# A linear-attention kernel with a feed-forward layer: another order of its opening, other due times, and sums of k times v with 48 weight columns

## The chip, the cores and the metric

The kernel runs on one core of a Trainium2 chip. The metric is the device time of one execution in microseconds (us). The five engines of the core are TensorE (PE in the profile, its weight loads PEld), VectorE (DVE), ScalarE (ACT), GpSimd (POOL) and SyncE (SP), which here issues the DMAs.

## The reference

Four batches (B), eight heads (H), 768 positions (S) and head size 48 (D). First a gated recurrence for each batch and head, then a feed-forward layer with squared relu on 3072 tokens, model size 384 and inner size 2048:

```python
state = np.zeros((B, H, D, D))
for t in range(S):
    state = alpha[:, :, t, :, None] * state + np.einsum('bhd,bhe->bhde', k[:, :, t], v[:, :, t])
    y[:, :, t] = np.einsum('bhd,bhde->bhe', q[:, :, t], state)
x = y.transpose(0, 2, 1, 3).reshape(B * S, H * D)
h = np.maximum(x @ w_in, 0.0)
out = h * h @ w_out
```

The inputs of the recurrence are float32; the two weight matrices come as 8 bytes a number and are converted to float32 in the kernel.

## The kernel before, in words

**Blocks.** The recurrence is cut into chunks of 128 positions. A block n is one chunk of one batch; there are 24 blocks, and four of them (one chunk of all four batches) make a group g, so there are six groups. The feed-forward layer runs on a group of 512 tokens at a time.

**Attention of a block.** `ln` takes the logs of alpha and `cs` (L288 to L292) sums them along the chunk on TensorE. `eb` and `ei` make the exponentials b and 1/b, and `mq`, `mk` (L314) multiply q and k with them. `qT`, `kT` (L355), or `turn` (tile T, L529) for later groups, transpose them on TensorE; `qc`, `kc` copy the result out (L371, L537). `scores` (sc, L418) forms the products of q and k, `state_sums` (kv, L441) the sums of k times v, both into the same two PSUM banks (tile `sckv`). `masked` (am, L426) and `sums_copied` (us, L452) take them out on VectorE, `next_state` (st, L466 and L467) forms the new state, scaled with the last row of b. For the first four blocks that row is turned on TensorE (`lt` L343, `lc` L349); for later ones it goes through memory: `bl` stores it and `br` (L333) loads it as tile `last`, both from SyncE's queue. The output y of two blocks (L398) is made in `ga` and `gb`, which also hold scores, sums, masks and the new state of the next two blocks: `ga` those of its first, `gb` those of its second. `ev` copies y into the columns of x (L562, on ScalarE, for a few on VectorE). Two heads share a tile of 128 rows: head e = 0 has rows 0 to 63, head e = 1 has rows 64 to 127; of each 64 only D = 48 are numbers of that head, the rest are zeros or unused.

**Feed-forward of a group.** Group 0 multiplies in plain float32: L931 for h (`ha`, `hb`: the two halves of the tokens), and L760 for the output. Later groups split weights and x into a near and a rest part and multiply in three passes (L681 for h; L843 and L855, in part still L760, for the output). The parts of the weights are made once (`prepare`), stored, and loaded again for each group; `room` bounds how many such tiles are held at a time. ScalarE and VectorE work up h: relu and square (L696, L594, L710 and others).

**Weights.** `load_weights` (L122 on SyncE) brings a raw piece of 768 KB; `convert_first` (L174, L178 on VectorE), `convert_middle` (L187, L190 on ScalarE) and `convert_second` (L196, L200, L203 on VectorE) turn it into float32. Words such as `first0`, `middle0` and `second0` in the order stand for these for piece 0.

**What sets the order.** Nothing is scheduled by a program at build time: each engine runs its instructions in the order in which the Python code records them. For the first four blocks and the first pieces of weights that order is a string of step names, recorded word by word. A word such as `load2a` issues a DMA on SyncE; words of different engines only order work that shares an engine. `zeros` records three float32 matmuls of zeros (L384) into a bank that nobody reads. After the string, `weave` mixes units of feed-forward work, each with a cost, with events that have a due time in the same units: the attention steps of later blocks, loads, weight splits. An event is recorded ahead of the first unit that begins at or after its due time. The due times are in the table `AT` and, relative to the start of a pair of blocks, in `PLAN`.

```python
def weave(units, events, at=0):
    for cost, f, args in units:
        while events and events[0][0] <= at:
            _, e, given = events.pop(0)
            e(*given)
        f(*args)
        at += cost
```

Of the kernel before, what the change touches and what calls it, by code (L numbers as in the profile page):

```python
# [15 lines left out]


GB = 4
AT = {'u0': 2, 'evs': 0.4, 'lead': 4, 'post': 3, 'w_first': (45.82, 44.44, 94.99), 'wstep': 2.31, 'w_in_at': 1.92, 'w_in_by': 3.02, 'room1': 25, 'room': 26, 's0': 3, 'ahead': 12, 'late': 23, 'xs': 0.35, 'g0': (-0.17, 20.59, 27.02), 'sc0': (2.36, 2.26, 2.42), 'g1': (7.68, 18.74, 27.21), 'g': (2.3, 15.42), 'g1x': 47.42, 'gx': 39.86, 'g0x': 55.51, 'k0': 2, 'h0': 16, 'k1': 5, 'h1': 0, 'h1by': 5, 'evs0': 0.23, 'tp': 'DDAD', 'tp1': 'AADD', 'split': 8, 'o0': (42.39, 46.35), 'o1': (), 'o2': (21.54, 19.65, 30.49, 26.1, 43.38, 50.96), 'str1': 14.0, 'ga': 9.32, 'gb': 12.97}


RUN = {0: 128, 32: 32, 64: 64, 96: 32}
# [3 lines left out]
def kernel(  # L26
# [13 lines left out]
    B, H, S, D = q.shape  # L40
    C = 128
    NCH = S // C
    NP = H // 2
# [4 lines left out]
    G = 64 - D  # L48
# [19 lines left out]
    s_t = [s_all.pop(0) for _ in range(B)]  # L68
# [30 lines left out]
    def tile_of(x, n):  # L99
        return lent.get((x, n), tiles[x][n % len(tiles[x])])  # L100
# [133 lines left out]
    last = consts.tile([128, 4, NP], FP32, name="last")  # L234
    nc.gpsimd.memset(last, 0.0)
    last_t = [last[:, i, :] for i in range(4)]
# [33 lines left out]

    SPLIT = AT["split"]

# [135 lines left out]
    HALF = [slice(0, 64), slice(64, C)]  # L408
# [26 lines left out]
    def state_sums(n):  # L435
        ps = two[n]
        for p in range(NP):
            for e in range(2):
                first = (2 * p + e) * D
                for h in range(1 if n // B == NCH - 1 else 2):  # L440
                    marks["k", n] = nc.tensor.matmul(  # L441
                        out=ps[h][64 * e : 64 * (e + 1), 1, p, G:64],
                        lhsT=tile_of("k", n)[HALF[h], 2 * p + e, :],
                        rhs=tiles["v"][n % NV][HALF[h], first : first + D],
                        start=True, stop=True, skip_group_check=True,
                    )

    def sums_copied(n):

        ps = two.pop(n)  # L450
        u = blk[n]["u"] = u_all[n % 3]
        nc.vector.tensor_tensor(  # L452
            out=own(u), in0=own(ps[0][:, 1]), in1=own(s_t[n % B]), op=ALU.add
        )
        blk[n]["kv1"] = own(ps[1][:, 1])

    def own(x):
        return x[:, :, G:64]

    def next_state(n):  # L460
        blk[n]["s"] = s_t[n % B]
        if n // B < NCH - 1:
            s_all.append(s_t[n % B])
            s_t[n % B] = s_all.pop(0)
            s, last = own(s_t[n % B]), last_t[n % 4].unsqueeze(2).to_broadcast([128, NP, D])
            nc.vector.tensor_tensor(out=s, in0=blk[n].pop("kv1"), in1=own(blk[n]["u"]), op=ALU.add)  # L466
            nc.vector.tensor_tensor(out=s, in0=s, in1=last, op=ALU.mult)  # L467

# [17 lines left out]
    def ga(a, n):  # L486

        if n is not None:
            for f in (scores, state_sums, masked, sums_copied):
                f(n)  # L490
        if a is not None:
            product = y_begin(a)
            for h in range(1 if a < B else 0, 2):
                for m, p, e in heads(a):
                    rows = slice(64 * e, 64 * e + D)
                    s = blk[m]["u" if h else "s"]
                    product(m, p, e, s[rows, p, G * (1 - e) : 64], blk[m]["qs"][rows, p, HALF[h]], HALF[h])


            for m, p, e in heads(a):  # L500
                end = inner(product, m, p, e, e)
            marks["y", a] = end
            passed = nc.gpsimd.nop(nofuse=True)
            dep(passed, end)
            two["y"] = product, passed
        if n is not None:
            next_state(n)

    def gb(a, n):

        if a is not None:
            product, passed = two.pop("y")
            for i, (m, p, e) in enumerate(heads(a)):
                begin = inner(product, m, p, e, 1 - e)
                if i == 0:
                    dep(begin, passed)
        if n is not None:
            for f in (scores, state_sums, masked, sums_copied, next_state):
                f(n + 1)
# [67 lines left out]
    here, todo, room = {}, [], [22]  # L587
# [37 lines left out]
    def diff_w(w, p):  # L625
# [7 lines left out]
        for x in "ld":  # L633
            t = made.pop((x, w, p))
            if w == "i" or p >= NW - AT["k0"] or (x == "l" and p >= NW - AT["k1"]):
                here[x, w, p] = t
        pump()

    def prepare(at, w, p):
        step = AT["wstep"]  # L640
        fs = (cast_w, rest_w, diff_w)
        return [(at + i * step, f, (w, p)) for i, f in enumerate(fs)]
# [78 lines left out]
    def splits_of_x(at, g):  # L721
        return [(at + i * AT["xs"], f, (g, i % KM)) for i, f in enumerate((split_x,) * KM + (diff_x,) * KM)]

    def layer_in(g):
        units = []
        for n in range(NJ + 2):
            if n < NJ:
                units.append((1.05, in_x, (n,)))
            if 0 <= n - 2 < NJ:
                units.append((0.53, in_y, (n - 2,)))  # L730
            if 0 <= n - AT["post"] < NJ:
                units.append((0, in_post, (n - AT["post"],)))
            if AT["lead"] <= n < AT["lead"] + AHEAD and (g > 1 or AT["k1"] == NW):
# [230 lines left out]

    steps = {f.__name__: f for f in (ln, sp, cs, eb, ei, mq, mk, bl, br, lt, lc, qT, qc, kT, kc, ev)}
    steps["sc"], steps["kv"], steps["am"] = scores, state_sums, masked
    steps["us"], steps["st"] = sums_copied, next_state
    steps["ya"], steps["yb"] = lambda n: ga(n, None), lambda n: gb(n, None)
# [5 lines left out]
    for x in "stky":  # L974
# [3 lines left out]
    steps["hb"] = lambda j: ffn_in(0, j, slice(HT, 2 * HT))  # L978
    steps["first"], steps["middle"], steps["second"] = convert_first, convert_middle, convert_second
    first = """  # L980
        zeros2 ln0 cs0 ln1 eb0 cs1 load0v ei0 mq0 mk0 load2a eb1 qT0 load3a qc0 mq1
        kT0 kc0 load1v ei1 qT1 mk1 load2k load2q qc1 sc0 kT1 weights0 kc1 kv0 load3q
        am0 lt1 sc1 ln2 us0 ln3 cs2 lt0 am1 load3k kv1 cs3 eb2 us1 ei2 gt1 mk2
        load2v weights1 ya0 mq2 yb0 lc1 gy0 eb3 kT2 lc0 load3v qT2 ei3 load4a zeros2
        st0 ea00 kc2 qc2 ed01 ed02 first0 zeros2 load4q mq3 zeros2 mk3 qT3 middle0
        qc3 kT3 second0 first1 kc3 lt3 lt2 sc2 kv2 am2 ea03 us2 sc3 kv3 gk3 middle1
        weights2 lc3 am3 us3 ha0 ya2 yb2 second1 weights3 ea20 lc2 ed21 ha1 ha3
        weights4 ed22 ed23 first2 st2 middle2 ha2 hb0 load4v hb1 st3 st1 load4k
    """
    for word in first.split():  # L990
        f = max((x for x in steps if word.startswith(x)), key=len)
# [2 lines left out]


    PLAN = (
        (-1.2, "ln0 ln1"),
        (-0.5, "sp0"),
        (0.0, "sp1"),
        (2.5, "cs0 cs1 eb0 ei0"),  # L1000
        (3.0, "eb1 ei1"),
        (3.5, "mk0"),
        (4.0, "bl0"),
        (4.5, "mq0 mk1 bl1"),
        (5.0, "mq1"),
        (6.5, "turn br1"),
        (7.0, "kc0 qc0 kc1 qc1 br0"),
        (9.5, "ga"),
        (10.5, "gb"),
    )  # L1010
    EARLY = (
        (0, "ln0"),
# [90 lines left out]
    for g in range(1, NG):  # L1103
        events = []
        if g + 1 < NG:
            n = GB * (g + 1) + 2
# [4 lines left out]
        if g == 1:  # L1111
# [5 lines left out]
            n = min(AT["k0"], AT["k1"])  # L1117
# [41 lines left out]
```

## Time and profile before

| | us |
|---|---|
| Median of 3 runs | 516.4 (515.83 to 516.55) |
| Span of the profiled execution, first to last instruction | 514.6 |
| TensorE busy | 508.3 |
| VectorE busy | 377.0 |
| ScalarE busy | 302.3 |
| GpSimd busy | 6.0 |

The profile holds one execution. Its own time is not listed beside it, only its span; the median lies 1.8 us above the span, and times in the text are made from the span and that difference. The mean granted TensorE clock was 1.000. The busy time of TensorE is the time in which at least one matmul was in flight; it does not say that each matmul is as short as it can be, and zeros count as busy like any other matmul.

A row of the chain in time has its start, its length, and the engine, tile and line (and x, the number of instructions). A row of the timeline has start, length, engine, line, operation, output <- input, shapes and count. A row of the groups has busy time, mean ns of one instruction, then idle time before it and what ended it. A row of the waits has who waited for whom: us in total, times, and the longest in us. A float32 matmul shows as two records of TensorE, except in the small tiles of scores, sums and y, where 16 matmuls show as 32.

### The profile page before, as it was taken

What the parts mean: (1) busy time and instruction counts of PE and PEld (TensorE: products, weight loads), DVE (VectorE), ACT (ScalarE), POOL (GpSimd) and SP (SyncE); (2) the same over time, 40 slices, a digit from 0 to 9 for tenths busy, and PEclk for the clock granted to TensorE, in tenths of its full rate; (3) what the DMA queues carried; (4) which work ended last, traced back from release to release, by engine and by line L of the source; (5) the groups of instructions that cost most, each with busy time, mean ns of one, the idle gap of its engine ahead of it and who ended that gap; (6) DMA issues with size and microseconds to landing.
All of it is one profiled execution on the core that took longest, in us unless ns stands there. A gap on an engine that the chain in (4) does not pass through costs nothing.

```text
span 514.6 us, 12773 instructions
## 1 busy us (share of the span) xinstructions
PE 508.3 (99%) x5166; PEld 404.6 (79%) x5166; DVE 377.0 (73%) x656; ACT 302.3 (59%) x627; POOL 6.0 (1%) x33
## 2 busy tenths in 40 slices
PE   8999999999999999999999999999999999999997
PEld 6884456669877679988888888888888888888996
DVE  3798899898789869886698286799275588274961
ACT  4789875677788576376764175855075663144520
POOL 4000000000000000000000000000000000000000
PEclk9999999999999999999999999999999999999999
DMA  9989867272797788799975678894775544789201
GB/s 171 226 238 269 233 177 226 33 224 101 267 238 199 189 188 234 263 330 222 241 187 154 209 220 229 222 225 146 227 221 168 186 128 151 214 277 401 88 0 63
DMA packets 144794, 102.73 MB, mean 200 GB/s; under 512 B 116560, under 2 KB 118240, under 8 KB 144736
## 3 DMA queue, kind: packets, MB, share of 16 engines
q1 hardware_dynamic: 144736, 101.92, 70.4%
q8 instruction: 41, 0.67, 0.6%
q14 instruction: 17, 0.14, 0.1%
HBM read 84.57 MB, written 17.33 MB: 198 GB/s over the span
## 4 chain that ended last, share of the span: by engine, by line
PE 96%; DMA 2%; SPq 1%; DVE 1%; issue 0%; ACT 0%; DVEq 0%; POOLq 0%
PE h L681 31%; PE o L760 22%; PE o L843 13%; PE h L931 8%; PE o L855 6%; PE y L398 4%; PE sckv L418 3%; PE T L529 2%; PE sckv L441 2%; PE cs L288 1%; DMA a_in<-in_alpha_dram 1%; PE zeros L384 1%; DMA last<-row 1%; PE cs L291 1%; SPq L333 1%; PE cs L292 1%
## 5 line engine op out<-in xcount | busy, mean ns | idle before, releaser
L696 ACT ACTIVATE hid<-h 128x512 f32<-128x512 f32 x56 | 33.7, 601 | 88.4 <-PE h L681 86.7
L681 PE MATMUL h<-xd,wd 128*128 128x512 f32 x240 | 68.4, 398 | 0.0
L681 PE MATMUL h<-xa,wb 128*128 128x512 f32 x240 | 67.8, 391 | 0.0
L681 PE MATMUL h<-xl,wl 128*128 128x512 f32 x240 | 67.6, 390 | 0.0
L594 DVE TENSOR_TENSOR hid<-h,hid 128x512 f32<-128x512 f32 x56 | 38.5, 689 | 33.9 <-PE h L681 33.6
L562 ACT COPY x<-y 32x256 f32<-32x256 f32 (+1 forms) x137 | 48.9, 365 | 8.7 <-PE y L398 6.4
L681 PEld LDWEIGHTS h<-xl,wl 128*128 128x128 f32 x240 | 45.0, 188 | 9.6
L681 PEld LDWEIGHTS h<-xa,wb 128*128 128x128 f32 x240 | 44.9, 188 | 9.4
L681 PEld LDWEIGHTS h<-xd,wd 128*128 128x128 f32 x240 | 43.7, 188 | 9.2
L760 PE MATMUL o<-w_out,hid 128*128 128x384 f32 x144 | 48.9, 492 | 0.0
L931 PE MATMUL h<-x,w_in 128*128 128x512 f32 (+1 forms) x120 | 43.0, 511 | 0.0
L655 ACT ACTIVATE ha<-hid 128x512 fp32r<-128x512 f32 x42 | 26.7, 638 | 26.1 <-DVE hx L656 12.8
L760 PEld LDWEIGHTS o<-w_out,hid 128*128 128x128 f32 x144 | 26.7, 190 | 17.2
L710 DVE SCALAR_TENSOR_TENSOR hid<-hid 128x512 f32<-128x512 f32 x56 | 37.8, 684 | 0.0
L931 PEld LDWEIGHTS h<-x,w_in 128*128 128x128 f32 x120 | 22.4, 190 | 16.9 <-issue 13.9
L855 PE MATMUL o<-hd,wd 128*128 128x512 f32 x144 | 33.4, 391 | 0.0
L656 DVE SCALAR_TENSOR_TENSOR hl<-ha,hid 128x512 fp32r<-128x512 f32 x42 | 28.8, 686 | 4.7 <-ACT ha L655 4.4
L855 PEld LDWEIGHTS o<-hd,wd 128*128 128x128 f32 x144 | 26.8, 188 | 6.1 <-ACT o L848 0.6
L594 DVE TENSOR_TENSOR hd<-ha,hl 128x512 fp32r<-128x512 f32 x42 | 29.1, 692 | 1.9
L843 PE MATMUL o<-hx,wb 128*128 128x512 f32 x72 | 28.4, 394 | 0.0
L843 PE MATMUL o<-hx,wl 128*128 128x512 f32 x72 | 28.0, 389 | 0.0
L843 PE MATMUL o<-ha,wb 128*128 128x512 f32 x72 | 28.0, 389 | 0.0
(130 smaller groups left out, 950.4 us busy)
## 6 DMA issues: line engine op xcount, KB each, us to landing
wd<-do SPq DMA_DIRECT2D x37, 384.0 KB
wl<-lo SPq DMA_DIRECT2D x34, 384.0 KB
wl<-li SPq DMA_DIRECT2D x32, 384.0 KB
wd<-di SPq DMA_DIRECT2D x32, 384.0 KB
raw<-in_moe_w_in_dram SPq DMA_DIRECT2D x8, 768.0 KB
raw<-in_moe_w_out_dram SPq DMA_DIRECT2D x8, 768.0 KB
v_in<-in_v_dram SPq DMA_DIRECT2D x24, 192.0 KB
a_in<-in_alpha_dram SPq DMA_DIRECT2D x22, 192.0 KB
```

The costliest lines, as they stand in the source:

```text
L398: ins = nc.tensor.matmul(out=ys[e][64 * half : 64 * half + D + G * e, m % 2, p // 2, t], lhsT=lhsT, rhs=rhs, start=(half, e) not in seen, ...
L562: copy(out=x[kk][to : to + m, t : t + 2], in_=blk[n]["y"][e][r : r + m, :, p // 2],)
L594: nc.vector.tensor_tensor(out=o, in0=x, in1=z, op=op)
L655: nc.scalar.activation(out=a, in_=x, func=AF.Copy, scale=NEAR * E)
L656: nc.vector.scalar_tensor_tensor(out=l, in0=a.bitcast(FP32), scalar=-1.0 / E, in1=x, op0=ALU.mult, op1=ALU.add)
L681: nc.tensor.matmul(out=acc["h", j], lhsT=here[w, "i", p][:, kk, jj * 128 : (jj + 1) * 128], rhs=x_parts[x][:, kk], start=start and kk == 0 ...
L696: nc.scalar.activation(out=hid[j], in_=x, func=AF.Copy, scale=E)
L710: nc.vector.scalar_tensor_tensor(out=h, in0=h, scalar=0.0, in1=h, op0=ALU.max, op1=ALU.mult)
L760: nc.tensor.matmul(out=acc[t][:, 0:DM], lhsT=lhs[:, t * C : (t + 1) * C], rhs=rhs, start=start, stop=stop, skip_group_check=True,)
L843: nc.tensor.matmul(out=acc[c], lhsT=by_parts(here[w, "o", p], jj, c), rhs=x, start=n == 0 and w == "b", stop=n == NJ - 1 and w == "l", ski ...
L855: nc.tensor.matmul(out=acc[c], lhsT=by_parts(here["d", "o", p], n % 2, c), rhs=h_diff[n], start=False, stop=last and n == NJ - 1, skip_gro ...
L931: nc.tensor.matmul(out=ps, lhsT=w[:, kk, c0 : c0 + 128], rhs=xT[g][kk][:, cols], start=(kk == 0), stop=(kk == KM - 1),)
```

## The change

- **The opening's string.** The same steps in another order, with two words `zeros2` less (four become two, so twelve filler matmuls become six). The loads of SyncE come in the order a0 q0 k0 a1 q1 k1 v0 v1 q2 a2 a3 k2 raw0 q3 k3 raw1 v2 v3 a4 raw2; before it is a0 q0 k0 a1 q1 k1 v0 a2 a3 v1 k2 q2 raw0 q3 k3 v2 raw1 v3 a4 q4 raw2. `first1` now comes before `second0`.
- **Due times.** Many values of `AT` and five rows of `PLAN` change: among them `turn` from 6.5 to 6.99, `ga` from 9.32 to 10.09 and the bounds `room1` and `room` from 25 and 26 to 24.
- **The sums of k times v.** The second head of a pair (e = 1) takes 48 columns of k as weights instead of 64, so it writes rows 64 to 111 instead of 64 to 127. VectorE's steps on the sums and states (L452, L466, L467) take 112 partitions instead of 128.

```diff
-AT = {'u0': 2, 'evs': 0.4, 'lead': 4, 'post': 3, 'w_first': (45.82, 44.44, 94.99), 'wstep': 2.31, 'w_in_at': 1.92, 'w_in_by': 3.02, 'room1': 25, 'room': 26, 's0': 3, 'ahead': 12, 'late': 23, 'xs': 0.35, 'g0': (-0.17, 20.59, 27.02), 'sc0': (2.36, 2.26, 2.42), 'g1': (7.68, 18.74, 27.21), 'g': (2.3, 15.42), 'g1x': 47.42, 'gx': 39.86, 'g0x': 55.51, 'k0': 2, 'h0': 16, 'k1': 5, 'h1': 0, 'h1by': 5, 'evs0': 0.23, 'tp': 'DDAD', 'tp1': 'AADD', 'split': 8, 'o0': (42.39, 46.35), 'o1': (), 'o2': (21.54, 19.65, 30.49, 26.1, 43.38, 50.96), 'str1': 14.0, 'ga': 9.32, 'gb': 12.97}
+AT = {'u0': 2, 'evs': 0.5, 'lead': 5, 'post': 3, 'w_first': (41.0, 46.62, 98.0), 'wstep': 2.4, 'w_in_at': 1.95, 'w_in_by': 2.89, 'room1': 24, 'room': 24, 's0': 2, 'ahead': 11, 'late': 23, 'xs': 0.13, 'g0': (-0.17, 20.59, 27.32), 'sc0': (2.35, 2.26, 2.45), 'g1': (6.25, 18.12, 27.21), 'g': (2.83, 13.94), 'g1x': 50.81, 'gx': 38.48, 'g0x': 56.05, 'k0': 2, 'h0': 15, 'k1': 5, 'h1': 2, 'h1by': 7, 'evs0': 0.29, 'tp': 'DDAD', 'tp1': 'AADD', 'split': 8, 'o0': (40.99, 48.51), 'o1': (), 'o2': (21.44, 19.65, 30.49, 28.56, 43.81, 48.78), 'str1': 15.07, 'ga': 10.09, 'gb': 12.97}
...
-                first = (2 * p + e) * D
+                first, wide = (2 * p + e) * D, D if e else 64
...
-                        out=ps[h][64 * e : 64 * (e + 1), 1, p, G:64],
-                        lhsT=tile_of("k", n)[HALF[h], 2 * p + e, :],
+                        out=ps[h][64 * e : 64 * e + wide, 1, p, G:64],
+                        lhsT=tile_of("k", n)[HALF[h], 2 * p + e, 0:wide],
...
     def own(x):
-        return x[:, :, G:64]
+        return x[0 : 64 + D, :, G:64]
...
-        zeros2 ln0 cs0 ln1 eb0 cs1 load0v ei0 mq0 mk0 load2a eb1 qT0 load3a qc0 mq1
-        kT0 kc0 load1v ei1 qT1 mk1 load2k load2q qc1 sc0 kT1 weights0 kc1 kv0 load3q
-        am0 lt1 sc1 ln2 us0 ln3 cs2 lt0 am1 load3k kv1 cs3 eb2 us1 ei2 gt1 mk2
-        load2v weights1 ya0 mq2 yb0 lc1 gy0 eb3 kT2 lc0 load3v qT2 ei3 load4a zeros2
-        st0 ea00 kc2 qc2 ed01 ed02 first0 zeros2 load4q mq3 zeros2 mk3 qT3 middle0
-        qc3 kT3 second0 first1 kc3 lt3 lt2 sc2 kv2 am2 ea03 us2 sc3 kv3 gk3 middle1
-        weights2 lc3 am3 us3 ha0 ya2 yb2 second1 weights3 ea20 lc2 ed21 ha1 ha3
-        weights4 ed22 ed23 first2 st2 middle2 ha2 hb0 load4v hb1 st3 st1 load4k
+        zeros2 ln0 ln1 cs0 eb0 cs1 ei0 mq0 load0v eb1 mk0 qT0 ei1 load1v mq1 qc0 kT0 load2q
+        load2a load3a kc0 qT1 mk1 load2k weights0 lt1 sc0 kT1 qc1 load3q kc1 am0 kv0 ln2
+        ln3 lt0 sc1 kv1 cs2 am1 us0 us1 cs3 ei2 gt1 load3k eb2 weights1 eb3 lc1 load2v ya0
+        yb0 lc0 gy0 ei3 load3v mk2 kT2 mq2 first0 qT2 ea00 load4a st0 kc2 qc2 weights2 mq3
+        lt3 ed01 qT3 zeros2 ed02 middle0 mk3 load4q kT3 lc3 first1 second0 kc3 load4v qc3
+        ea03 middle1 lt2 sc2 kv2 sc3 kv3 am2 ha0 us2 am3 us3 gk3 second1 ya2 yb2 weights4
+        lc2 ea20 ed21 ha1 ed22 ed23 st2 load4k weights3 first2 middle2 ha3 ha2 st1 hb1 hb0
+        st3
...
-        (-1.2, "ln0 ln1"),
-        (-0.5, "sp0"),
-        (0.0, "sp1"),
+        (-1.84, "ln0 ln1"),
+        (-0.24, "sp1"),
+        (0.22, "sp0"),
...
-        (4.5, "mq0 mk1 bl1"),
+        (4.37, "mq0 mk1 bl1"),
...
-        (6.5, "turn br1"),
+        (6.99, "turn br1"),
...
-        (10.5, "gb"),
+        (10.25, "gb"),
```

More of the change, by code (lines that the diff above doesn't have):

```diff
@@ L464, in next_state @@
             s_t[n % B] = s_all.pop(0)
-            s, last = own(s_t[n % B]), last_t[n % 4].unsqueeze(2).to_broadcast([128, NP, D])
+            s, last = own(s_t[n % B]), last_t[n % 4][0 : 64 + D].unsqueeze(2).to_broadcast([64 + D, NP, D])
             nc.vector.tensor_tensor(out=s, in0=blk[n].pop("kv1"), in1=own(blk[n]["u"]), op=ALU.add)
```

## Prediction

> **What bounds the kernel now.** I read the page's head first, then the chain in time through the opening, the opening's timeline, the groups by form, and at last the waits.
>
> ```profile
> PE 508.3 (99%) x5166; PEld 404.6 (79%) x5166; DVE 377.0 (73%) x656; ACT 302.3 (59%) x627; POOL 6.0 (1%) x33
> PEclk9999999999999999999999999999999999999999
> PE 96%; DMA 2%; SPq 1%; DVE 1%; issue 0%; ACT 0%; DVEq 0%; POOLq 0%
> ```
>
> TensorE is the path: it is busy 99% of the span at the full granted clock, and 96% of the chain is its own work. So an edit counts only where it takes PE work away, or a stretch in which PE stands or is kept busy with filler. The chain in time shows that the opening has such filler:
>
> ```profile
> 18.92 3.89 PE zeros L384 x18
> ...
> 24.29 0.62 PE sckv L418 x32
> ...
> 25.37 0.48 PE sckv L418 x32
> ...
> 26.30 1.49 PE h L931 x6
> ```
>
> The zeros row is work whose output nobody reads. The next rows of the timeline show what runs beside it:
>
> ```profile
> 20.00 0.54 DVE L174 TENSOR_SCALAR power<-raw 128x768 uint32<-128x768 uint32 x1
> 24.09 0.96 DVE L203 TENSOR_TENSOR w_in<-w_in,power 128x768 f32<-128x768 f32 x1
> 24.97 0.55 DVE L174 TENSOR_SCALAR power<-raw 128x768 uint32<-128x768 uint32 x1
> 26.02 0.78 DVE L426 COPY_PREDICATED am<-halves_mask,sckv 128x256 f32<-128x256 uint32 x2
> ```
>
> The first FFN matmul (26.30) needs the weights that L203 ends at 25.05, and the y of blocks 2 and 3 needs the masks from 26.02 on. VectorE is the second path of the opening, right behind PE.
>
> **Zeros.** Six of the twelve filler matmuls go, all from this run (nine become three): twelve of its 18 records, 12 x 0.216 (3.89/18) = 2.59 us. That is a gain only if the first FFN matmul and the masks come earlier, which VectorE decides; so the next part carries the price.
>
> **The opening's order.** Up to about 16 us I walk the new order with the old durations: am0 now lies ahead of kv0, which starts at 12.1 for 11.66; sc1, kv1, cs2 and cs3 then follow each other at their old lengths and the first y starts at 15.97, before 15.91. No cost: the transposes of the row sums (lt) went into a PE gap. a2 and a3 land some 2 us later (three 192 KB loads at about 1.0 us each stand ahead, two of them were behind), about 13 and 14; cs2 and cs3 begin after 14, so that is covered, with under 1 us to spare.
> From 18 us VectorE is laid end to end. The first part of raw0's conversion (L174, L178) can start at 18.24, as raw0 lands at 18.19 (before it was started at 20.00). Then st0, mq3, three x copies (1.33), mk3 and lc3 follow, to 22.35. Now the order has L174 and L178 of **raw1** ahead of the second part of raw0 (L196, L200, L203): 0.46 + 0.56 + three at 0.88 to 0.96, so L203 ends t + 3.80, t being the later of 22.35 and raw1's landing. Before raw1 was issued at 17.92 and landed at 24.36; now its issue follows k3 directly, near 14.2, and v2 is behind it. k3 landed at 19.76; raw0 and raw1 added 2.5 to 3.5 us each to the load ahead of them. So raw1 lands at 22.3 to 23.3, and the first FFN matmul starts at 26.2 to 27.1, before 26.30 (26.23 in the timeline). am2 keeps its place behind L203, so y moves with it. Bounds: -0.1 and +0.9 us; a wait of 0.2 us on the x copies at 34.6 us falls away if all comes later. I take +0.5, the middle, since raw0 was nearer 3.5 on its slowest part and 2.5 on most. So the 2.59 us are not gained: they turn into PE time without filler, 18 to 26 us.
>
> **The narrow weights.** 704 sums matmuls become half 64, half 48 columns wide. What a narrower load is worth shows in y, which already mixes both:
>
> ```profile
> L441 PEld LDWEIGHTS sckv<-v_in,k_in 64*64 64x64 f32 x672 | 13.2, 135 | 0.2 <-issue 0.2
> L398 PEld LDWEIGHTS y<-am,v_in 64*64 64x64 f32 x384 | 13.5, 134 | 0.0
> L398 PEld LDWEIGHTS y<-am,v_in 64*48 64x48 f32 x384 | 12.6, 120 | 4.2 <-issue 3.7 <-POOLq L503 0.5
> ```
>
> One 48-column load takes 120 ns, one of 64 134: 14 ns less. But the tiles of the array load side by side, each at a pace of its own: in a run of y at 16.5 us the 64-wide pair begins a load every 58 ns, the 48-wide pair beside it every 56, and the run ends with the slower. So it spans 422 ns from first to last load, as do the all-64 scores (423); these sums take 428. The change narrows one pair of the sums (e = 1) and leaves the other. [...] I take 0, the y rows being nearest. VectorE's 112 partitions for 128 save nothing: x copies of 16, 32, 48 and 64 partitions take 361 to 367 ns alike.
> [...]
>
> **Attention steps of later groups.** The new due times join two sections of group 1:
>
> ```profile
> 67.86 0.62 PE sckv L418 x32
> 68.48 0.45 PE sckv L441 x32
> 68.94 2.77 PE h L931 x6
> 71.71 0.63 PE sckv L418 x32
> ```
>
> Now the second pair follows the first, and the six matmuls of h come after. By the starts in the timeline, scores to second sums take 4.36 us (67.79 to 72.15), 1.79 without 2.57 for h; the same three runs side by side in the opening take 1.45 (24.22 to 25.67). Gain 0.35 us (0 if the steps are split again elsewhere). All other sections only move between matmuls of the same kind.
> What is left are waits of PE. Before has three that a move touches: at 144.2 the transposes T stand 0.20 us for q times b (L314, 144.00 to 144.55); nine L681 matmuls now lie between, some 2 us, so it goes. At 181.5 T stands 0.4 us for the bank that the x copies (L562, to 182.2) empty; T comes two L760 (0.65 us) later, the copies are 0.1 unit further apart, so 0.4 goes. At 238.2:
>
> ```profile
> DVE s L467 <- DMA last<-row: 10.0, 3, 4.2
> ```
>
> ```profile
> 233.06 3.86 DMA last<-row
> ...
> 237.31 0.68 DVE hid L710
> 238.00 0.61 DVE hid L594
> 238.61 0.04 issue
> 238.66 0.68 PE sckv L418 x28
> ```
>
> VectorE's state step waits for a row that comes through memory; behind it queue two FFN steps, and the scores need the bank that the second one empties: 0.45 us. The step (in ga) moves from 9.32 to 10.09 units, past such FFN steps, while the row's DMAs (br0) stay at 7.0: they run before the wait, and 0.45 goes. Each of these is 0 to its full length: together 0 to -1.05, taken in full, as in the rows around I find the released work early enough. Of moves that I cost at nothing (weight splits w_first, o0, o2; casts; loads; 24 kept tiles for 26), ScalarE (59%) and VectorE (73%) have room, and each us of a late step would be a PE us.
>
> **Sum.** 0.5 - 0.35 - 1.05 = -0.9 on a span of 514.6: 513.7. The three runs have a median of 516.4, 1.8 above the profiled span; so 515.5. About 0.2% (1.03 us) is what a measurement of this kernel tells from no change, and 515.4 is the line for faster.
>
> **Rivals.**
> - Early raw1: it lands by 22.8 or before, the opening costs 0 to +0.2, and the time is about 515.0. For: most parts of raw0 took 2.5 us. With the forecast this is one mechanism; 0.26 here, 0.31 for raw1 late (515.2 to 515.9).
> - The narrow loads pay: -2.05 more, 513.5. For: the 14 ns. Against: the 64-wide pair sets the pace. 0.10.
> - The conversion isn't last: if only 0.8 of the 2.59 us of filler comes back, because the walk has VectorE too late, -0.9 - 0.5 - 0.8 = -2.2, 514.2. Against: each VectorE row there is back to back. 0.08.
> - Slower, the rows: place, SyncE's queue ahead of the state steps. The DMAs of a row pass the weight streams, whose issue waits for a free tile, and 24 tiles for 26 in the later groups makes those waits longer. The three waits above total 10.0 with a longest of 4.2, so near 4.2, 2.9, 2.9; PE lost 0.45 at the longest, so the cover is 3.75. With every row 1.5 us later they are 5.7, 4.4, 4.4 and cost 1.95 + 0.65 + 0.65 = 3.25. In place of the -0.45 that is +2.8: sum +2.35, 518.8. It decides from 1.1 us on, where the sum passes +1.0. For: the row's first DMA stood 1.92 us in SyncE's queue at 230.1. Against: ga's later place gives 1 us more cover. 0.20.
> - Slower, the clock: PE now stands in pieces of up to 1.9 us between 18 and 26 us. At the start matmuls of this size begin every 427 ns (1.7 to 5.5 us), in the long run of filler every 216. A fall to half speed that lasts as long as it did there, 4.4 us, over the first FFN run and y (1.49 + 1.42 + 0.69 and what follows) costs half of it, 2.2: sum +1.3, 517.7. It decides from 1.9 us of cost on. The row of clocks has no such drop. 0.05. [...]
>
> **Numbers.** Faster 0.26 + 0.10 + 0.08 = 0.44; same 0.31; slower 0.20 + 0.05 = 0.25. Range: 513.6 leaves out most of the narrow loads; 517.6 the worse part of the rows. The likeliest case alone is 514.9 to 516.4.
>
> **What would show it.** In the profile after: zeros x6 beside a first h L931 between 26.2 and 27.1 with L203 ending just before; raw1 landing at 22.3 to 23.3; L441 runs at about 0.43 us; no PE wait at T near 144 and 181 or at the scores near 238; a PEclk row of nines. I am wrong if h L931 begins before 25.5, if L441 runs take under 0.36, or if `s L467 <- DMA last<-row` grows above 12 us.

## The result, and the profile after

The changed kernel is slower: 520.25 us median of 20 runs (517.77 to 526.54), against 516.39 for the kernel before; the ratio is 1.0077, with a 95% interval from 1.0055 to 1.0099. The forecast was 515.5. Its runs also spread over 8.8 us, those of the kernel before over 4.2 (515.77 to 519.96). Ratios, here and below, leave out runs in a slower state of the chip (one of these 20, 526.54 us) and compare with runs of the kernel before on the same chip.

Part of the spread goes with the clock. Of the other 19 runs, seven show a mean granted clock of 0.990 to 0.997 and take 521.0 to 525.5 us; the remaining twelve (0.998 or more) have a median of 519.2. Of the kernel before, no run whose clock is on record shows less than 0.998. The profiled execution spans 520.1 us, before 514.6. It took 522.57 us at a clock of 0.999, the longest of the twelve, so its trace shows more loss than a usual run has. From the page of the profile after:

```profile
PE 506.6 (97%) x5154; PEld 402.4 (77%) x5154; DVE 377.1 (72%) x656; ACT 301.5 (58%) x627; POOL 6.0 (1%) x33
PE 89%; DVE 3%; SPq 2%; DMA 2%; ACT 2%; issue 2%; DVEq 0%; POOL 0%; POOLq 0%
q8 instruction: 41, 0.67, 0.6%
```

TensorE is busy for 1.7 us less than before (508.3) in a span that is 5.5 us longer, so it stands 7 us more. The chain lost seven points of PE, and 2% are "issue", time in which an engine waits for nothing that the profile shows. The chain in time through the opening says where (start, length, what; `...` stands for rows left out):

```profile
16.02 0.89 PE y L398 x41
16.91 1.75 issue
18.66 0.57 PE y L398 x15
...
27.27 1.53 PE h L931 x6
28.81 0.81 PE y L398 x38
29.62 1.71 issue
31.33 0.61 PE y L398 x23
```

In the kernel before, the first of these two y ran through:

```profile
15.99 1.12 PE y L398 x62
```

Twice TensorE now stops in the middle of a y, with no semaphore that the profile shows it to wait for. From the start of one instruction of TensorE to that of the next it is 1.97 and 1.92 us, and pauses and waits of TensorE are given in this way from here on; in a run of 512-column matmuls of L681 0.23 us of such a length is the matmul itself. A third such pause, 1.25 us, comes at 394.9, and a fourth, 0.30 us, at 336.7. The list of waits (engine, line, released by: total, times, longest) has them as well; before, the first line read 5.8 in all and 0.5 at the longest, and the second was missing:

```profile
PEld y L398 <- issue: 9.5, 16, 1.9
PE y L398 <- issue: 4.5, 3, 1.8
```

What "issue" hides is told by the third line of the page above, and by the single transfers behind it, whose times are in the packet records of the trace. Queue q8 brought 41 transfers of 16,384 bytes; TensorE has 10,482 records in this trace, 255.7 for each transfer, so I take one transfer for 256 instructions, a **piece** of its program; that q8 is TensorE's is read from this count, no view says it. Counting TensorE's records in order of start, all four pauses come after record 193 of a block of 256 (records 449, 961, 7,873 and 8,897), and so does the one pause of 0.36 us in the kernel before, at 169.9 us (record 3,777):

```profile
169.21 0.95 PE y L398 x60
170.15 0.15 issue
170.30 0.79 PE y L398 x31
```

In each case the transfer of the next piece ended 1.2 to 1.5 us before TensorE went on. The same holds where nothing stops: if the transfers are counted off against the pieces in order, none of the 600 pieces in the 15 traces of this document begins less than 1.23 us after its transfer ended. I read this as a TensorE that had used up its piece before the next one was there to be run. The traces show the times; the experiments bear on the reading.

Against the kernel before, the changed one is 2.5 us late by the 40th record of L931 (39.88 for 37.36). Along the way it wins back 0.35 us at the joined sections, 0.15 near 144, 0.4 by 172 (where the kernel before has its pause and this one has none), 0.35 at the transposes T near 182 and 0.6 by 242, so 0.6 us are left. Then it loses again: 1.9 us by 273, most of it in one wait at 270.6, 0.5 near 322, 0.35 by 338 and 1.25 at 395 (two of the pauses), 0.4 at 461.5, where weights come late, and 0.4 behind the last matmul.

### The profile page after: what moved, and what is told of

It is laid out like the page before. It is cut to its first block, busy times and chain, and to the rows that moved or that the text cites. A ratio compares the mean times of both kernels' runs of the same rounds, so it can differ in the third digit from the quotient of the medians.

```text
span 520.1 us, 12743 instructions
## 1 busy us (share of the span) xinstructions
PE 506.6 (97%) x5154; PEld 402.4 (77%) x5154; DVE 377.1 (72%) x656; ACT 301.5 (58%) x627; POOL 6.0 (1%) x33
## 4 chain that ended last, share of the span: by engine, by line
PE 89%; DVE 3%; SPq 2%; DMA 2%; ACT 2%; issue 2%; DVEq 0%; POOL 0%; POOLq 0%
PE h L681 28%; PE o L760 21%; PE o L843 11%; PE h L931 8%; PE o L855 6%; PE y L398 4%; PE sckv L418 2%; PE T L529 2%; PE sckv L441 2%; SPq L879 1%; PE cs L288 1%; DMA wd<-di 1%; DVE hd L594 1%; DMA last<-row 1%; PE warm L244 1%
## 5 line engine op out<-in xcount | busy, mean ns | idle before, releaser
L681 PE MATMUL h<-xa,wb 128*128 128x512 f32 x240 | 69.1, 396 | 0.4 <-DVE hid L594 0.4
L681 PE MATMUL h<-xl,wl 128*128 128x512 f32 x240 | 67.7, 390 | 0.0
L681 PE MATMUL h<-xd,wd 128*128 128x512 f32 x240 | 67.2, 393 | 0.2 <-DMA wd<-di 0.2
L594 DVE TENSOR_TENSOR hid<-h,hid 128x512 f32<-128x512 f32 x56 | 38.4, 688 | 39.2 <-PE h L681 32.7
L681 PEld LDWEIGHTS h<-xl,wl 128*128 128x128 f32 x240 | 45.0, 188 | 9.8
L681 PEld LDWEIGHTS h<-xd,wd 128*128 128x128 f32 x240 | 44.5, 188 | 9.6 <-ACT hid L719 0.6
L681 PEld LDWEIGHTS h<-xa,wb 128*128 128x128 f32 x240 | 44.1, 188 | 9.8 <-DVE hid L594 0.5
L931 PE MATMUL h<-x,w_in 128*128 128x512 f32 (+1 forms) x120 | 42.8, 510 | 0.0
L710 DVE SCALAR_TENSOR_TENSOR hid<-hid 128x512 f32<-128x512 f32 x56 | 37.7, 683 | 0.0
L656 DVE SCALAR_TENSOR_TENSOR hl<-ha,hid 128x512 fp32r<-128x512 f32 x42 | 28.8, 686 | 10.7 <-ACT ha L655 10.7
L931 PEld LDWEIGHTS h<-x,w_in 128*128 128x128 f32 x120 | 22.5, 190 | 16.6 <-issue 14.1
L594 DVE TENSOR_TENSOR hd<-ha,hl 128x512 fp32r<-128x512 f32 x42 | 29.1, 692 | 2.7 <-PE o L843 0.9
L843 PE MATMUL o<-hl,wl 128*128 128x512 f32 x72 | 28.2, 392 | 1.3 <-DVE hl L656 1.3
L843 PE MATMUL o<-ha,wb 128*128 128x512 f32 x72 | 28.4, 395 | 0.0
L843 PE MATMUL o<-hx,wl 128*128 128x512 f32 x72 | 28.2, 391 | 0.0
```

The source lines that it names most:

```text
L594: nc.vector.tensor_tensor(out=o, in0=x, in1=z, op=op)
L656: nc.vector.scalar_tensor_tensor(out=l, in0=a.bitcast(FP32), scalar=-1.0 / E, in1=x, op0=ALU.mult, op1=ALU.add)
L681: nc.tensor.matmul(out=acc["h", j], lhsT=here[w, "i", p][:, kk, jj * 128 : (jj + 1) * 128], rhs=x_parts[x][:, kk], start=start and kk == 0 ...
L710: nc.vector.scalar_tensor_tensor(out=h, in0=h, scalar=0.0, in1=h, op0=ALU.max, op1=ALU.mult)
L843: nc.tensor.matmul(out=acc[c], lhsT=by_parts(here[w, "o", p], jj, c), rhs=x, start=n == 0 and w == "b", stop=n == NJ - 1 and w == "l", ski ...
L931: nc.tensor.matmul(out=ps, lhsT=w[:, kk, c0 : c0 + 128], rhs=xT[g][kk][:, cols], start=(kk == 0), stop=(kk == KM - 1),)
```

## The experiments

**1. The narrow weights alone.**

```diff
 kernel before
-    lhsT=tile_of("k", n)[HALF[h], 2 * p + e, :],
+    lhsT=tile_of("k", n)[HALF[h], 2 * p + e, 0:wide],   # wide = D if e else 64; own() 112 partitions
```

> The kernel before with the 48-column weights of the second head and the 112-partition steps alone; order and due times as before. Theory fetch (TensorE stands in the runs of small tiles because the next piece of its program has not arrived; the change moved the piece ends and the loads they compete with): the number of TensorE instructions and all loads are as before, so 516.4, same within 1 us. Theory narrow (the mixed widths of 64 and 48 columns cost time in the sums): slower by 2 us or more, and the sums' runs of 32 records take over 0.5 us for 0.45. Theory order (the new order and due times alone make it slower): 516.4.

Measured: 516.21 us for 516.56, ratio 0.9999 (0.9983 to 1.0014). The narrow columns bring no gain or loss that can be told from noise. In the traces most runs of the sums on their own take 0.40 us from the start of the first matmul to that of the last, before 0.415: some 13 ns a run, so 0.3 us in 22 runs.

**2. The new order of the opening alone.**

```diff
 kernel before, with the opening's string of the changed kernel
```

> The kernel before with the new order of the opening alone (six filler matmuls less, loads in the new order); 64 columns and the due times as before. Theory fetch: the two pauses of TensorE of 1.9 us inside y (at 16.7 and 29.4 us) appear again at the same instructions, with no semaphore behind them, and the first FFN matmuls after them come some 2.5 us later than before; 518 to 519.5, more where the moved piece ends bring further pauses. Theory order (the conversion on VectorE alone makes the opening late): no pause inside y, the opening +0.5 to +1, 517. Theory plan (the later due times cost it): 516.4.

Measured: 519.57, ratio 1.0065 (1.0039 to 1.0091). Both pauses are there at records 449 and 961, of 2.50 and 1.66 us, and the 40th record of L931 is 2.4 us late. The opening makes some three of the four us.

**3. The old order of the opening in the changed kernel.**

```diff
 changed kernel, with the opening's string of the kernel before
```

> The changed kernel with the order of the opening of before (twelve filler matmuls, loads in the old order); 48 columns and the new due times stay. Theory fetch: no pause in the first 35 us; of the profile after, +2.5 us are gone, the gains near 72, 144, 181 and 238 us stay and so do the new waits of VectorE near 272 and 322; the pause at 394.9 moves, as each piece ends 24 instructions earlier: 516.5 to 518. Theory plan: 519 to 521, as the opening has no part in it. Theory order: 515.5, the forecast without the opening.

Measured: 517.36, ratio 1.0011 (0.9994 to 1.0027). No pause comes in the first 35 us and none near 395. So the due times, forecast at -1.4, come out between nothing and slightly slower. New waits of TensorE show at 238.6 (0.77), 268.6 (0.86) and 318.8 us (1.39); experiments 8 and 12 are about the first and the last.

**4. Other places for the ends of the pieces.**

```diff
 changed kernel, first word zeros2 of the opening
-        for _ in range(3): matmul(zeros, 128x256)
+        for _ in range(2): matmul(zeros, 128x256)
+        for _ in range(17): matmul(zeros, 64x48)      # 64 more instructions
```

> The changed kernel with 64 more TensorE instructions at its start: the first three filler matmuls become two, and 17 matmuls of 64 x 48 into the same unread bank follow, about as long together. Every piece of 256 instructions now ends 64 instructions earlier in the work. Theory fetch: pauses without a semaphore come only after record 193 of a piece of 256 TensorE records, as in the profiles so far, which now is 64 records earlier in the work: none after the same y matmuls at 16.7 and 29.4 us and none at 394.9; there may be others. The time changes by 1 us or more either way, 516.5 to 522. Theories order and plan: the pauses, if they count at all, stay at the same work, and the time stays 520.3 within 1 us.

Measured: 524.61 (4 runs, 522.95 to 533.1), ratio 1.0150 (1.0110 to 1.0189), above the range expected. The pauses moved with the count, not with the work: they are again at records 449 and 961, which now lie 64 instructions earlier in the work (1.58 and 0.73 us). That of 394.9 is gone, and a new one of 1.41 us stands in another y, at record 4,545. The chain in time (y is L405 in this kernel):

```profile
190.22 1.23 PE y L405 x77
191.44 1.20 issue
192.64 0.45 PE y L405 x11
```

Without the 64 instructions this y runs through. So the number of instructions ahead sets where a pause can come, and a theory by which the work itself or its data make the pause does not fit. The time did not follow the pauses: the three largest add up to 3.7 us here and to 5.1 before this edit. Waits for semaphores came or grew at 306 (1.07) and 322 us (2.12), and three of the four runs show a clock of 0.987 to 0.996. So this run tells where pauses come, not what each costs.

**5. raw0 one load sooner, in the kernel before.**

```diff
-    load2k load2q qc1 sc0 kT1 weights0 kc1
+    load2k weights0 load2q qc1 sc0 kT1 kc1
```

> The kernel before with one word of its opening moved: the load of the first raw piece of weights (raw0) is issued ahead of that of q of block 2, some 1.1 us earlier (10.5 us for 11.6); TensorE's instructions are the same in number and order. Theory fetch (the next piece of TensorE's program is brought by the same DMA engines and waits behind a raw load that was issued before the piece before it ended, at about 12 us): the piece comes at 15 to 16 us for 14.2 and TensorE pauses 0.5 to 2 us inside the first y at 16.5 us, at the same record 449; 517 to 518.5. Theory order (only what VectorE converts and when counts): raw0 lands 1 us sooner, no pause, 515.5 to 516.5.

Measured: 519.04, ratio 1.0042 (1.0025 to 1.0058). One load moved by one place, TensorE's program untouched, and the pause is there. First the load on SyncE in the timeline, then the chain, then one stretch of the table by windows, whose columns are its length and the busy time of PE, PEld, DVE, ACT and POOL, then the granted clock, the share of the DMA engines and GB/s:

```profile
10.43 0.99 SPq L122 DMA_DIRECT2D raw<-in_moe_w_in_dram  x1
```

```profile
15.92 0.84 PE y L398 x45
16.76 1.89 issue
18.65 0.54 PE y L398 x14
```

```profile
19.00:22.40 3.40, 3.29 (x50) 3.02 (x43) 1.69 (x5) 1.63 (x5) 0.00 (x0) 0.50 0.93 258
```

The pause is 2.10 us from start to start, and after it the granted clock was at half for 3.41 us, which adds up to 1.7 us to the loss (half of the 3.41, an estimate).

**6. raw2 later, in the changed kernel.**

```diff
-    weights2 mq3 ... sc3 kv3 am2
+    mq3 ... sc3 kv3 weights2 am2
```

> The changed kernel with one word of its opening moved: the load of the third raw piece (raw2, 21.9 us in the profile after) is issued behind the sums of block 3, some 4 us later. Theory fetch: the piece of TensorE's program that is asked for at 24.5 us no longer waits 3.7 us behind raw2, but 1 to 2 us, and the pause of 1.9 us in y at 29.4 us is gone or under 0.4; the pause at 16.7 us stays; 520.3 - 1.7 = 518.6. Theory order: no gain, 520.3, or slower by what the third piece's conversion comes later.

Measured: 518.00, ratio 1.0026 (1.0010 to 1.0042): some 2 us of the loss are gone with one word. The second y runs through (chain in time; before this edit 1.71 us of issue stood inside it):

```profile
27.83 1.20 PE y L398 x61
29.02 0.03 issue
```

The pause in the first y stays, 1.43 us, and yet the 40th record of L931 begins at 36.97, 0.4 us sooner than in the kernel before. So up to there the new order is no loss in itself. The run as a whole still takes 1.7 us more; in its trace TensorE stands 1.81 us at 317.6 for L594 behind the splits L279 and L280, the queue that experiment 12 is about.

**7. raw0 later as well.**

```diff
 late_raw2
-    load2k weights0 lt1 ... load3k eb2 weights1
+    load2k lt1 ... load3k weights0 eb2 weights1
```

> As late_raw2, and the load of the first raw piece too is issued later, behind k of block 3 (about 12.9 us for 11.4), so after the end of the first piece of program that matters (12.2 us). Theory fetch: no pause at 16.7 us either (the piece waits 1 to 2 us for 3.6); the first FFN matmul then starts when L203 ends, which raw1's landing at 22 us sets, so 0.5 to 1 us more than late_raw2 gives: 517.6 to 518.1. Theory order: raw0 lands 1.5 us later, so the conversion and the time are 0 to 1.5 us later than in the changed kernel, 520.3 to 521.8.

Measured: 520.22, ratio 1.0060 (1.0036 to 1.0084). A miss. The first pause fell to 0.32 as expected, but VectorE stood for raw0 (now landing at 19.67), q of block 3 is queued behind that, TensorE's transposes waited 2.7 us at 19.2, and what follows came 2 us later. With that the piece's end fell behind the issue of raw2 again (26.75 for 25.36), and the second pause returned, 2.11 us; the granted clock was at half for 3.41 us after 21.6.

**8. The splits of the logs later.**

```diff
 old_opening
-        (-0.24, "sp1"),
-        (0.22, "sp0"),
+        (1.0, "sp1"),
+        (0.8, "sp0"),
```

> The changed kernel with the order of the opening of before (as old_opening, 517.4), and the two splits of the logs (L279, L280, sp0 and sp1) due at 0.8 and 1.0 instead of 0.22 and -0.24; only VectorE's order differs from old_opening. Theory queue (in the later groups the four split steps, 1.9 us, queue between the state step that waits for its row and the FFN step that empties the bank TensorE needs): the waits of TensorE at 238.6 (0.77 us) and 318.8 (1.39 us) in old_opening go or fall under 0.4: 515.3 to 516.2. Rival, that the rows themselves come too late: the waits stay, 517.4.

Measured: 518.46, ratio 1.0040 (1.0027 to 1.0052). The waits at 238 and 319 went as expected, but 0.93 us came at T (182.0), 0.59 and 0.69 us at the sums of logs (137 and 321.5), which now wait for the splits, and two pauses at piece ends, 0.56 us (101.3) and 0.60 (192.9). The time missed the expectation and settled nothing.

**9. The filler alone.**

```diff
 kernel before
-    load4a zeros2 st0 ... first0 zeros2 load4q
+    load4a st0 ... first0 load4q
```

> The kernel before with six of its filler matmuls left out (those in the run at 18.9 us) and nothing else changed, loads included. Theory fetch: the piece ends at records 449 and 961 and the loads before them stay where they were (the fillers lie between them, and later pieces end 24 instructions later in the work), so no pause over 0.3 us before 35 us; VectorE sets the first FFN matmul as before: 516.4 within 0.7 us. A rival, that the filler is what kept TensorE ready and its removal itself makes the loss (clock or order): 518 to 519.5, with pauses in y or a lower clock. A second rival, that TensorE was the bound there: 513.8 to 515.

Measured: 517.07, ratio 1.0020 (1.0008 to 1.0031). The 40th record of L931 begins at 37.43 for 37.36: 2.59 us of TensorE's work were taken out of the opening and nothing came of it. No pause over 0.2 us lies before 35 us; but at 170.2 us, record 3,777, the pause of 0.36 us has become 1.03, since the piece ends 24 instructions later in the y. That is as much as the 0.7 us by which the median is higher; the profiled span alone is 0.2 us longer.

**10. The sums of block 0 ahead of its mask.**

```diff
 late_raw2
-    am0 kv0
+    kv0 am0
```

> As late_raw2 (raw2 loaded later, 518.0), and the mask of block 0 goes back behind the sums of block 0, as in the kernel before, so the sums start at 11.5 to 11.7 us for 12.0 and the piece of program that ends in them is asked for some 0.45 us earlier, while raw0 is issued at 11.4 as it was. Theory fetch: the next piece is less behind raw0 and comes at 14 to 15 us for 15.3; the pause in the first y falls from 1.43 us to 0 to 0.9: 516.5 to 517.5. Theory order: 518.0, within 0.5 us.

Measured: 518.33, ratio 1.0032 (1.0012 to 1.0051). The piece came at 13.76 us for 15.26 and the pause fell from 1.43 to 0.61, as expected; the time did not follow (516.5 to 517.5 was expected). In the profiled run TensorE stood 2.13 us at 317 us for VectorE, and the clock then fell to half for 3.41 us. So what the first pause costs in the changed kernel was not isolated; in the kernel before, experiment 5 shows a loss of 2.8 us with one such pause and, in its profile, a slow stretch behind it.

**11. Two of the due times alone.**

```diff
 kernel before
-        (6.5, "turn br1"),
+        (6.5, "br1"),
+        (6.99, "turn"),
-'ga': 9.32
+'ga': 10.09
```

> The kernel before with two due times of the change alone: the transposes T (turn, 6.5 to 6.99) and ga (9.32 to 10.09); the row's DMAs, the splits of the logs, the opening and the weights stay. Theory queue (the forecast's later part was right in itself, and other due times gave it back by putting the log splits between the state step and the FFN step): the waits of TensorE at 144 (0.20), 181 (0.4) and 238 (0.45) go and none over 0.3 comes: 515.3, and no more than 0.4 of it lost to a pause at a piece's end, as no instruction is added. Rival, that moving ga by itself makes other waits as long: 516.4 or slower.

Measured: 515.90 (12 runs), ratio 0.9991 (0.9981 to 1.0001); the span is 513.8, 0.8 less than before, and 0.36 of that is the pause at 169.9, which is gone here. The waits at 144 and 238 us are gone and 0.35 of 0.4 us is left near 181; a pause of 0.50 us came at a piece's end at 191.8, where a matmul alone takes 0.32. The gain in the median, 0.43 us, is not clear of noise. With raw0 issued one load later, behind q of block 3:

```diff
 turn_ga
-    kT1 weights0 kc1 kv0 load3q
+    kT1 kc1 kv0 load3q weights0
```

> As turn_ga (two due times of the change on the kernel before, 515.9), and the load of the first raw piece issued one load later, behind q of block 3 (about 12.0 us for 11.5), so after TensorE has come to the end of its piece of program in the sums of block 0 (11.7 us). TensorE's instructions are the same. Theory fetch: the next piece no longer waits behind raw0, comes at 12.3 to 13.3 us for 13.7, and the pause of 0.18 us at 16.3 us goes, in the profiled run and by as much or more in runs where it is longer: 515.4 to 515.9. Theory order: raw0 lands 0.5 us later, before VectorE takes it at 20 us, so no change: 515.9.

Measured: 515.89, ratio 0.9988 (0.9977 to 0.9999). The piece comes at 13.41 us for 13.71 and the pause of 0.18 us at 16.3 us is gone; a wait of 0.65 us for a state row came at 237.9, and the median stayed. This is the one version whose interval lies below the kernel before, by 0.12% (0.01 to 0.23).

**12. The starts of the pairs, on top of turn_ga.**

```diff
 turn_ga
-        (-1.2, "ln0 ln1"), (-0.5, "sp0"), (0.0, "sp1"),
+        (-1.84, "ln0 ln1"), (-0.24, "sp1"), (0.22, "sp0"),
-'g': (2.3, 15.42)
+'g': (2.83, 13.94)
```

> turn_ga (515.9) with three more of the change's due times: the logs (ln, sp rows of the plan) and the starts of the pairs of blocks in the later groups (g from 2.3 and 15.42 to 2.83 and 13.94). The opening, the weights, the instructions of TensorE and their number stay. Theory queue: the four split steps L279, L280 now lie on VectorE between the state step that waits for its row and the FFN step L594 that empties the bank TensorE needs, as in the changed kernel, so waits of TensorE for L594 of 0.6 to 2 us come near 237 and 318 us: 517 to 518.5. Rival, that these due times cost nothing and other ones of the change (weight splits, 24 kept tiles) gave the gain back: 515.9, no such waits.

Measured: 521.60 (4 runs), ratio 1.0087 (1.0065 to 1.0109), above the 517 to 518.5 expected. TensorE stands 1.03 us at 240.2 and 3.12 at 319.8, each time for L594, with the clock at half for 6.83 us after the second. The queue that makes it, in the chain of the changed kernel itself, where it cost 0.63 us:

```profile
319.25 0.69 DVE hid L710
319.93 0.28 DVE hi L279
...
320.71 0.36 DVE hi L279
...
321.10 0.56 DVE lo L280
321.66 0.61 DVE hid L594
```

Ahead of these stands the state step L467, which waits for its row. In the kernel before only L710 stood between it and L594. Now the splits of the next pair, which starts 1.48 units sooner, come in between, and TensorE waits for all of them. This is shown for this queue; how much of the rest is due to 24 kept tiles and the other weight times stays open.

**When a piece comes late.** The runs together give a scale. A raw load of 768 KB is issued by SyncE at a certain time. "Begins" is the start of the first instruction of the piece in hand; the expectations take about this time for the one when the next piece is "asked for", an estimate, as no trace shows when it is (over the whole trace after, transfers start between 6.6 us before this point and 5.4 us after it). Then come the wait until the transfer of the next piece starts, counted from "begins", and the pause where the piece in hand is used up. All are in us.

| kernel | raw0 issued before "begins" | wait for the transfer | pause |
|---|---|---|---|
| late_raw02 | -1.05 | 1.93 | 0.32 |
| turn_ga_raw0 | -0.48 | 1.41 | 0 |
| before | 0.48 | 2.13 | 0 |
| kv_first | 0.65 | 1.98 | 0.61 |
| opening_alone | 1.13 | 3.97 | 2.50 |
| late_raw2 | 1.15 | 2.98 | 1.43 |
| after | 1.34 | 3.55 | 1.97 |
| early_raw0 | 1.57 | 3.86 | 2.10 |

These are raw0 and the first y. For raw2 and the second y it is the same: before -1.64 and a wait of 1.24 us, after 2.84 and 3.66. Where the raw load was issued over 1 us earlier, the wait was 1 to 2 us longer; that the load is what holds the piece is shown by experiments 5 and 6, which move it alone. The transfer takes 1.0 to 1.4 us and TensorE goes on 1.2 to 1.5 us after it, so this piece is 4.0 to 6.7 us in coming, while the one in hand is used up in 3.9 to 4.6. Where no raw load runs, at 168 us in the kernel before, it came in 3.0 us (0.61 + 0.94 + 1.43) while the piece in hand was used up in 2.6, hence the 0.36 us.

## Why the prediction was wrong, by its steps

**What bounds.** Right: TensorE sets the end and filler is no gain by itself. The step "the 2.59 us are not gained" is shown by no_zeros, in the old order.

**The opening's order, +0.5 with bounds -0.1 and +0.9.** This step failed. The walk on VectorE nearly held: L203 ended at 27.13, 4.4 us after raw1's first step for the 3.80 worked out (0.52 of it a wait for ScalarE's L187), and the first FFN matmul began at 27.27, 0.2 past the bound. raw1 landed at 22.07, a little sooner than said. But "the walk" priced the new order of the loads only by when their data land. It missed other transfers, those of q8 (0.6% of the span of the 16 DMA engines), which I read as TensorE's own program, and so two pauses of 1.9 us; the opening alone measures +3.0 us (519.57 for 516.56). The bound of +0.9 came from VectorE alone and held no price for a wait without a semaphore, though the trace of before had one, the 0.36 us at 169.9, with one q8 transfer just ahead of it. The prediction does not mention it.

**The narrow weights, 0.** Right, within 0.3 us. No run shows the 2.05 us that the rival takes off for narrow loads: a load of the narrowed pair takes 121 ns for 135, but a whole run of the sums takes only 13 ns less (0.402 us for 0.415), about the difference of one load, as fits the pair that stays 64 wide (135 ns) setting the pace. The x copies quoted for VectorE's partitions are rows of ScalarE; the reading held all the same, as L466 and L467 take 0.36 us with 128 partitions and with 112.

**The joined sections, -0.35.** Right: the lag falls from 2.52 to 2.17 us across them.

**The three waits, -1.05.** Each was read rightly: all three waits are gone or shorter in the profile after. In turn_ga the span is 0.8 us shorter, while the median falls by 0.43 us with an interval that reaches no change. But "moves that I cost at nothing" failed: the earlier start of the second pair put four splits into the queue that had just been relieved. In the changed kernel TensorE stood 0.63 us for it, in splits_pairs 4.2 us. VectorE's 73% share said nothing of it. What made the 1.7 us at 270.6, where L843 waits for L656 at the end of a full queue on VectorE, was not tried.

**The rivals.** The rows were not the mechanism: the waits for them fell,

```profile
DVE s L467 <- DMA last<-row: 8.4, 4, 3.7
```

but the place was near, since it is what stands behind a row that costs. The clock stayed full in the profile after, but not in all runs: with seven of 19 at 0.990 to 0.997, this rival is part of the loss, about 0.7 us of the median (519.9 over the 19, 519.2 over the twelve). In the profiles of four experiments the clock fell to 0.50 just after TensorE had stood, for 2.10 to 3.12 us. The rival had about the right price (2.2 us; half of 3.41 is 1.7), but looked for the standing in gaps without filler; it came from the program's pieces and from VectorE's queue. Of the three signs that were to show me wrong, none came up: a list of signs of the known terms says nothing of a missing one.

## What to carry to other kernels

In the changed kernel, raw loads issued 1.34 and 2.84 us before a piece began went with pauses of 1.97 and 1.92 us. Where small matmuls use up 256 instructions in 2 to 5 us, as here, find the ends of the pieces and try the large loads in another place than just ahead of them. 64 instructions more (pad64) or 24 less (no_zeros) moved the later ends, so judge such an edit on several runs and look for pauses with no semaphore. And when a wait is relieved, read again which instructions queue between it and the one that frees the next engine.

## What the runs showed of the hardware that I had not expected

- **TensorE's program seems to come by 41 transfers of its own, and data can make them late.** q8 brought 41 transfers of 16,384 bytes for 10,482 records of TensorE. With raw0 issued one place sooner (early_raw0) the wait for one of them grew from 2.13 to 3.86 us. In the long runs of 512-column matmuls this cost nothing, as the transfer had ended up to 28 us before its piece began (28.4 in the profile after, in L681); in the small tiles TensorE stood up to 2.50 us between two pieces (opening_alone).
- **After a pause of 2 us the clock was at half in some traces.** In early_raw0, kv_first and late_raw02 TensorE stood 2.10, 2.13 and 2.73 us, and the granted clock was then 0.50 for 3.41 us; in splits_pairs it stood 3.12 us and the clock was 0.50 for 6.83. In the profile after, pauses of 1.97 and 1.92 us left it at 1.00, and in opening_alone one of 2.50 did too, so length alone does not tell these apart. Where the pause lies does, in these traces. In each of the 15 traces every change of the clock comes a whole number of steps of 3.413 us after its first rise (in the kernel before, the fall at the end comes 508.59 us after it, 149 steps, in the profile after 512.00, 150 steps; in early_raw0 the changes are at 5.35, 19.00 and 22.42 us: four steps and one). In the step just before each of the four falls that come ahead of the last matmul, TensorE had no matmul in flight for 1.77 us (splits_pairs), 1.89 (early_raw0), 1.91 (kv_first) and 2.18 (late_raw02); in no other step between the first rise and the last matmul of any trace was that more than 1.59. The pause of opening_alone fell on both sides of a step's end, 1.28 and 1.11. The first rise came 4.2 to 7.3 us into the span (5.90 before, 7.32 after), so I take it that the same pause can come with a slow stretch in one run and not in the next. That would fit the spread of the runs; no experiment tested it.
